# The first layer's beginning in a four-layer kernel: another load order, another engine for two norms, masks later

## The chip, the cores and the metric

The kernel runs on one core of a Trainium2 chip. The core has five engines that run side by side, each through its own instruction list in order: TensorE (PE, matrix products; its weight loads are listed as PEld), VectorE (DVE), ScalarE (ACT), GpSimd (POOL) and SyncE (SP), which here only issues DMA transfers. The metric is the device time of one execution in microseconds (us), the median of three runs.

## What is computed

A sequence of 2048 tokens with 576 features passes four layers, attention (A) and MLP (B) in turn, twice, with the same weights each time. Each layer adds its result to x.

```python
def _A_ref(x, wqkv, wo):            # linear attention, 32 heads of 18
    qkv = (x @ wqkv) -> q, k, v per head
    phi = lambda t: jnp.where(t > 0, t + 1, jnp.exp(t)) + 1e-6
    pq, pk = phi(q), phi(k)
    kv = jnp.einsum("bhsd,bhse->bhde", pk, v)
    z = jnp.einsum("bhsd->bhd", pk)
    num = jnp.einsum("bhqd,bhde->bhqe", pq, kv)
    den = jnp.einsum("bhqd,bhd->bhq", pq, z)[..., None] + 1e-6
    return (num / den) @ wo

def _B_ref(x, w1, b1, w2, b2):      # MLP, 576 -> 4608 -> 576
    h = _gelu(_layernorm(x) @ w1 + b1)
    return h @ w2 + b2

x = x + _A_ref(_layernorm(x), A_wqkv, A_wo)
x = x + _B_ref(_layernorm(x), B_w1, B_b1, B_w2, B_b2)
x = x + _A_ref(_layernorm(x), A_wqkv, A_wo)
x = x + _B_ref(_layernorm(x), B_w1, B_b1, B_w2, B_b2)
```

The layer norm subtracts the mean of a row and divides by the root of its variance plus 1e-5. Inputs, weights and the output are bfloat16.

## The kernel before

The 2048 tokens are 16 tiles of 128 rows. Weights stay in on-chip memory for the whole run. Between layers x lies in a scratch tensor x_d in HBM.

**The norm pipeline.** `LNPipe` takes a tile through numbered stages, one stage for each call of `tick`: statistics on DVE (L229, L230: half a row each; L232 joins them to mean and variance, ln_mv; L235 adds eps, ln_u), the power -0.5 on POOL (L242, ln_rstd), the product -mean * rstd on DVE (L246, ln_nmr), the normalised tile (L254 on ACT, or L258 on DVE or POOL) into one of four buffers `y_ring`, with a copy of its last 64 columns into the 64 pad columns on POOL (L260), and five transposes on PE (L267) whose result ACT (L269) or DVE (L271) copies to yT.

The features are 4.5 blocks of 128. The last block of yT has 64 true rows and 64 that come from the pad columns; in attention the weights' rows against the pad are zero (L158), in the MLP the pad is a second copy of the last 64 features.

**First half of an attention layer.** For each tile t, `kv_proj` computes the key products (L336, two halves into k_ps), phi of them (ACT reads k_ps twice, L289 and L291; DVE ends it, L292 and L294), and the value products (L344, L347 into v_ps, of which there is one buffer). ACT (L349) and DVE (L351) copy v_ps to `v_ring`, which frees it for the next tile. `kv_acc` adds tile t-1 to kvacc (L360). From t = 4 on, one query product (L366) is done for each tile. In the first layer `pre_a1_layer0` runs ahead of each tile: it loads and feeds tile t + LEAD, ticks the pipeline, and issues one piece of the later weights (`late_pieces`: wo, b1, nine of w1, six of w2).

**Second half.** Denominators, the product with wo (L450), and for each tile the residual sum on DVE (L316), its store to x_d, and a prefetch of the next x tile (L301: xbf, from the input in the first layer; L304: xo, from x_d, in the others). One group in five has its scaling on POOL (L442). Tiles of the next layer enter the norm pipeline here; those after the first four are read back from x_d (L224).

**Masks.** `build_masks` fills six constant tiles on POOL by memsets and affine selects. It is called once, by `late_pads`, at t = 2 of the first layer; the masks are first read after the last key and value product.

**What sets the order.** A scheduler places each engine's instructions by data dependence and priority; the order in the program is a wish. `chained` makes the DMAs that pass through it keep their order on SP. Each DMA also takes one of eight completion semaphores in turn, and waits until the DMA eight places earlier has landed. From the ninth tile of the first layer on, `pe` keeps PE in program order.

At the start PE runs 14 products of zeros (L157) on `ident`, which POOL has built, so that its clock is up when the first tile comes.

Of the kernel before, what the change touches and what calls it, by code (L numbers as in the profile page):

```python
# [15 lines left out]
P = 128  # L16
# [16 lines left out]
NWARM = 14  # L33


def build(tc, A_x, A_wqkv, A_wo, B_w1, B_b1, B_w2, B_b2, out, dbg=None, n_layers=4):
    nc = tc.nc
    dbg = dbg or {}
    with ExitStack() as ctx:
# [26 lines left out]
        act_dummy = const.tile([P, 1], F32, name="act_dummy")  # L66

        def build_masks():
            sel = nc.gpsimd.affine_select
            nc.gpsimd.memset(maskz[:], 1.0)  # L70
# [6 lines left out]
            nc.gpsimd.memset(z_row[:], 0.0)  # L77
            nc.gpsimd.memset(eps_row[:], 1e-6)
            nc.gpsimd.memset(one_row[:], 1.0)
            nc.gpsimd.memset(act_dummy[:], 0.0)  # L80
            sel(out=z_row[:], in_=z_row[:], compare_op=ALU.not_equal, fill=1.0,
                base=-126, pattern=[[0, 1]], channel_multiplier=1)
            nc.gpsimd.memset(head_sel[:], 1.0)
# [4 lines left out]
            nc.gpsimd.memset(quad_mask[:], 1.0)  # L88
# [4 lines left out]
            nc.gpsimd.memset(head_bc[:], 0.0)  # L93
# [64 lines left out]
        nc.gpsimd.memset(wqkv_sb[64:P, 4, :], 0.0)  # L158
# [5 lines left out]
        def late_setup():  # L164
            build_masks()
# [26 lines left out]
        def piece_b2_dma():  # L192
            nc.sync.dma_start(out=b2_bc[:], in_=B_b2.partition_broadcast(P))
# [8 lines left out]
        state = dict(ycnt=0, vcnt=0)  # L202

        class LNPipe:
# [3 lines left out]
            def feed(self, xt, t, kind, norm_eng, evac_eng="dve", load_from=None):  # L208
                self.items.append(dict(stage=(0 if load_from is None else -1), xt=xt, t=t, kind=kind,
                                       norm=norm_eng, evac=evac_eng, load=load_from))  # L210
# [4 lines left out]
            def tick(self, transposes=1):  # L215
                for it in list(self.items):
# [9 lines left out]
                    elif st == 0:  # L226
                        xt = it["xt"]
                        stt = work.tile([P, 2, 6], F32, name="ln_st", bufs=4)
                        nc.vector.bn_stats(out=stt[:, 0, :], in_=xt[:, 0:HALF])  # L229
                        nc.vector.bn_stats(out=stt[:, 1, :], in_=xt[:, HALF:D])  # L230
# [13 lines left out]
                    elif st == 2:  # L244
# [4 lines left out]
                    elif st == 3:  # L249
                        y = y_ring[state["ycnt"] % NY]  # L250
                        state["ycnt"] += 1
                        xt = it["xt"]
                        if it["norm"] == "act":
                            nc.scalar.activation(out=y[:, 0:D], in_=xt[:, 0:D], func=ACT.Identity,  # L254
                                                 scale=it["rstd"][:, 0:1], bias=it["nmr"][:, 0:1])
                        else:
                            eng = nc.vector if it["norm"] == "dve" else nc.gpsimd
                            eng.tensor_scalar(out=y[:, 0:D], in0=xt[:, 0:D], scalar1=it["rstd"][:, 0:1],  # L258
                                              scalar2=it["nmr"][:, 0:1], op0=ALU.mult, op1=ALU.add)
                        nc.gpsimd.tensor_copy(out=y[:, D:DPAD], in_=y[:, 4 * P:D])  # L260
                        it["y"] = y
                    elif st == 4:
                        y = it["y"]
                        t = it["t"]
                        tp = ps_tp.tile([P, KD, P], BF16, name="tp", tag="tp")
                        for k in range(KD):
                            pe(nc.tensor.transpose(out=tp[:, k, :], in_=y[:, k * P:(k + 1) * P], identity=ident[:]))  # L267
# [355 lines left out]
        def pre_a1_layer0(t):  # L623
# [85 lines left out]
```

## Time and profile before

| | |
|---|---|
| median of 3 runs | 812.3 us (812.2 to 812.8) |
| the profiled execution | 816.66 us, of which 814.7 us are the span of the trace |
| PE busy | 785.2 us (96%) |
| ACT, DVE, POOL busy | 352.2, 259.2, 120.6 us |
| first key product (L336) starts | 15.01 us |
| first value product (L344) starts | 17.95 us |
| query products end, second half begins | about 84 us |
| first MLP product (L549) starts | 128.98 us |

The span runs from the first to the last recorded instruction of the profiled execution. "Busy" is the time in which an engine executes an instruction; an idle time before an instruction is put down to whatever released it, and is named behind it in brackets. Times in the trace are us from the span's start.

### The profile page before, as it was taken

To read this page: it belongs to the slowest core of one execution; us is meant where nothing else is said; L and a number is where in the kernel's file an instruction comes from. 1 tells how busy PE (TensorE), PEld (TensorE's weight loads), DVE (VectorE), ACT (ScalarE), POOL (GpSimd) and SP (SyncE) were. 2 spreads that over 40 slices of the span, in tenths; PEclk is the share of its full clock that TensorE was granted. 3 is DMA by queue.
4 is the path that set the end of the run, shared out by engine and by line. 5 is a ranking of instruction groups with operands and counts; after the bars stand their busy time and mean duration, and the time that the engine had idled before them with its cause. 6 is when DMAs were issued, how large, how long until landed. Compare 5 with 4: busy or idle time off the path is not lost.

```text
span 814.7 us, 16146 instructions
## 1 busy us (share of the span) xinstructions
PE 785.2 (96%) x6806; PEld 510.1 (63%) x6812; DVE 259.2 (32%) x764; ACT 352.2 (43%) x765; POOL 120.6 (15%) x218
## 2 busy tenths in 40 slices
PE   5999979999999999999999998799999999999998
PEld 3777554477458647845877765446854774585476
DVE  4675873024303502310345468621400310010000
ACT  4788844610640371066037787274046107403610
POOL 8440131012201201210100002220210110011000
PEclk8999999999999999999999999999999999999999
DMA  9990274002101201100110006820310110011000
GB/s 218 253 327 4 80 230 151 1 31 73 45 25 65 89 1 31 59 31 1 59 60 1 1 1 202 270 83 16 89 43 2 51 57 11 2 44 44 2 23 23
DMA packets 42898, 56.92 MB, mean 70 GB/s; under 512 B 10251, under 2 KB 26891, under 8 KB 42827
## 3 DMA queue, kind: packets, MB, share of 16 engines
q1 hardware_dynamic: 42826, 55.91, 22.6%
q8 instruction: 53, 0.87, 0.4%
q14 instruction: 19, 0.15, 0.1%
HBM read 39.38 MB, written 16.52 MB: 69 GB/s over the span
## 4 chain that ended last, share of the span: by engine, by line
PE 88%; DVE 3%; ACT 3%; DMA 2%; POOL 1%; issue 1%; SPq 0%; DVEq 0%; ACTq 0%
PE m_ps L596 35%; PE h_ps L549 19%; PE hp_ps L549 15%; PE q_ps L366 5%; PE k_ps L336 4%; PE v_ps L347 2%; PE wo_ps L450 2%; PE v_ps L344 2%; PE tp L267 2%; DMA xl<-x_d 1%; PE kvacc L360 1%; DVE xn L316 1%; ACT rden_bc L440 1%; DMA xbf<-in_A_x_dram 1%; POOL ln_rstd L242 1%
## 5 line engine op out<-in xcount | busy, mean ns | idle before, releaser
L596 PE MATMUL m_ps<-w_sb,hT 128*128 128x288 bf16 x2304 | 289.8, 286 | 0.0
L596 PEld LDWEIGHTS <-hT 128*128 128x128 bf16 x2304 | 223.2, 98 | 57.9 <-issue 3.4
L549 PEld LDWEIGHTS <-w_sb 64*128 64x128 bf16 x2304 | 124.4, 94 | 136.5 <-issue 1.7
L549 PE MATMUL hp_ps<-yT,w_sb 64*128 64x512 bf16 x1152 | 178.0, 376 | 0.0
L554 ACT COPY relay_sb<-relay_sb 128x1 f32<-128x1 f32 x144 | 28.5, 198 | 282.4 <-PE h_ps L549 239.4
L549 PE MATMUL h_ps<-yT,w_sb 64*128 64x512 bf16 x1152 | 147.9, 376 | 0.0
L545 ACT ACTIVATE hT<-h_ps,b1T 128x512 bf16<-128x512 f32 x144 | 91.0, 683 | 43.9 <-PE h_ps L549 43.9
L271 DVE COPY yT<-tp 128x640 bf16<-128x640 bf16 x40 | 19.6, 490 | 272.2 <-PE tp L267 272.2
L545 ACT ACTIVATE hT<-hp_ps,b1T 128x512 bf16<-128x512 f32 x144 | 91.1, 692 | 0.0
L242 POOL TENSOR_TENSOR ln_rstd<-ln_u,neg_half 128x1 f32<-128x1 f32 x64 | 35.2, 551 | 339.6 <-DVE ln_u L235 185.6
L306 POOL TENSOR_TENSOR xo<-xo,b_bc 128x576 f32<-128x576 f32 x32 | 40.8, 1275 | 154.1 <-DMA xo<-x_d 152.9
L450 PE MATMUL wo_ps<-kvwo,pq 126*128 126x288 bf16 (+1 forms) x320 | 49.3, 301 | 13.5 <-POOL pq L442 9.4
L549 PE MATMUL h_ps<-yT,w_tail 64*128 64x512 bf16 x144 | 54.1, 376 | 0.0
L549 PE MATMUL hp_ps<-yT,w_tail 64*128 64x512 bf16 x144 | 54.1, 376 | 0.0
L366 PE MATMUL q_ps<-yT,wqkv_sb 128*126 128x512 bf16 (+1 forms) x200 | 50.0, 382 | 0.5 <-ACT phi_a L291 0.5
L450 PEld LDWEIGHTS <-pq 126*128 126x128 bf16 (+1 forms) x320 | 31.7, 102 | 28.5 <-POOL pq L442 10.8
L316 DVE TENSOR_TENSOR xbf<-m_ps,xo 128x576 bf16<-128x576 f32 x16 | 12.1, 757 | 106.9 <-PE m_ps L596 106.9
L336 PE MATMUL k_ps<-wqkv_sb,yT 128*128 128x288 bf16 x320 | 45.9, 291 | 0.0
L289 ACT ACTIVATE phi_e<-k_ps 128x288 bf16<-128x288 f32 x64 | 27.3, 427 | 36.5 <-PE k_ps L336 36.5
L260 POOL COPY y_ring<-y_ring 128x64 bf16<-128x64 bf16 x64 | 15.8, 248 | 158.1 <-DVE y_ring L258 146.2
L292 DVE TENSOR_SCALAR phi_e<-phi_e 128x288 bf16<-128x288 bf16 (+2 forms) x104 | 28.7, 276 | 29.1 <-ACT phi_e L289 28.8
L549 PEld LDWEIGHTS <-w_tail 64*128 64x128 bf16 x288 | 27.1, 94 | 17.1
(94 smaller groups left out, 670.1 us busy)
## 6 DMA issues: line engine op xcount, KB each, us to landing
x_d<-xn SPq DMA_DIRECT2D x48, 288.0 KB, 2.2
xo<-x_d SPq DMA_DIRECT2D x48, 288.0 KB, 3.0
xl<-x_d SPq DMA_DIRECT2D x24, 288.0 KB, 2.9
w_sb<-in_B_w_dram SPq DMA_DIRECT2D x6, 864.0 KB, 9.1
w_sb<-in_B_w_dram SPq DMA_DIRECT2D x9, 512.0 KB, 4.9
x<-in_A_x_dram SPq DMA_DIRECT2D x16, 144.0 KB, 3.8
xbf<-in_A_x_dram SPq DMA_DIRECT2D x16, 144.0 KB, 3.7
out_dram<-xbf SPq DMA_DIRECT2D x16, 144.0 KB, 1.8
```

What stands on the lines that cost most here:

```text
L242: nc.gpsimd.tensor_tensor(out=rstd[:], in0=it["u"][:], in1=neg_half[:], op=ALU.pow)
L289: act_last["exp"] = nc.scalar.activation(out=e[0:rows, 0:n], in_=ps_ap, func=ACT.Exp).ins.name
L292: nc.vector.tensor_scalar(out=e[0:rows, 0:n], in0=e[0:rows, 0:n], scalar1=1.0, scalar2=1e-6, op0=ALU.min, op1=ALU.add)
L306: nc.gpsimd.tensor_tensor(out=xo[:], in0=xo[:], in1=b2_bc[:], op=ALU.add)
L316: nc.vector.tensor_tensor(out=xn[:].rearrange("p (h n) -> p h n", h=2), in0=halves, in1=xo[:].rearrange("p (h n) -> p h n", h=2), op=ALU.add)
L336: pe(nc.tensor.matmul(kp[:, 0:HALF], lhsT=yT[:, k, tok], rhs=wqkv_sb[:, k, D + half * HALF: D + (half + 1) * HALF], start=(k == 0), stop=( ...
L366: pe(nc.tensor.matmul(qp[0:GR[g], :], lhsT=wqkv_sb[:, k, GO[g]:GO[g] + GR[g]], rhs=yT[:, k, c * CA:(c + 1) * CA], start=(k == 0), stop=(k ...
L450: pe(nc.tensor.matmul(wp[:, half, 0:HALF], lhsT=pq[(g, c)][0:GR[g], j * P:(j + 1) * P], rhs=kvwo[g][0:GR[g], half * HALF:(half + 1) * HALF ...
L545: act_last["gelu"] = nc.scalar.activation(out=hT[f][:, 0:CB], in_=dst[n], func=ACT.Gelu_apprx_tanh, bias=b1T[:, f:f + 1], scale=1.0).ins.name
L549: mm = pe(nc.tensor.matmul(dst[n], lhsT=wt, rhs=mv, start=(seen[n] == 0), stop=(seen[n] == 8)))
L554: relay = nc.scalar.copy(out=relay_sb[:, 1:2], in_=relay_sb[:, 0:1])
L596: pe(nc.tensor.matmul(acc[:, half, 0:HALF], lhsT=hT[f][:, j * P:(j + 1) * P], rhs=w2_sb[:, f, half * HALF:(half + 1) * HALF], start=(f == ...
```

## The change

- Loads on SP: x0 and x1, the key weights, x2 and x3, the value weights, x4, and, after the first four tiles are fed, the query weights. Before, five x tiles came first, then key and value weights in one transfer, then the query weights. LEAD is 4 instead of 6. `pre_a1_layer0` still calls `load_x0` for tile t + LEAD without looking whether it is there.
- Late pieces (wo, b1, w1, w2) start at t = 2 instead of 0. The loads of b2 and of the first layer's residual tiles (L193, L301) join the chain of loads.
- Tiles 0 and 1 are normalised on DVE, the other 14 on POOL (before: four on ACT, twelve on POOL). The statistics of tiles 2 and 3 are tied to come after a DVE norm.
- Norms on DVE and POOL compute (x - mean) * rstd directly; the product -mean * rstd remains only for norms on ACT. A tile so normalised needs one stage less.
- The pad copy is done in the MLP only. The four y buffers are zeroed at the start on DVE, and so are the pad rows of the weights, formerly on POOL.
- `build_masks` is called at t = 6 and its fills are tied behind the latest norm on POOL.
- 10 products of zeros on a zeroed y buffer instead of 14 on `ident`; one activation at the start loads ACT's table.

```diff
-NWARM = 14
+NWARM = 10
...
-        def build_masks():
+        def build_masks(after):
             sel = nc.gpsimd.affine_select
-            nc.gpsimd.memset(maskz[:], 1.0)
+
+            def fill(tile_, value):
+                tc.add_manual_dep(nc.gpsimd.memset(tile_[:], value).ins, after, NOSYNC, reason="masks are not urgent")
+
+            fill(maskz, 1.0)
...
-        for t in range(5):
-            load_x0(t)
-        chained(nc.sync.dma_start(out=wqkv_sb[:, 0:4, D:3 * D],
-                                  in_=A_wqkv[0:4 * P, D:3 * D].rearrange("(k p) n -> p k n", p=P)))
-        chained(nc.sync.dma_start(out=wqkv_sb[0:64, 4, D:3 * D], in_=A_wqkv[4 * P:D, D:3 * D]))
-        chained(nc.sync.dma_start(out=wqkv_sb[:, 0:4, 0:D],
-                                  in_=A_wqkv[0:4 * P, 0:D].rearrange("(k p) n -> p k n", p=P)))
-        chained(nc.sync.dma_start(out=wqkv_sb[0:64, 4, 0:D], in_=A_wqkv[4 * P:D, 0:D]))
-        nc.vector.memset(y_ring[NY - 1][:], 0.0)
+        def load_wqkv(part):
+            cols = slice(part * D, (part + 1) * D)
+            chained(nc.sync.dma_start(out=wqkv_sb[:, 0:4, cols],
+                                      in_=A_wqkv[0:4 * P, cols].rearrange("(k p) n -> p k n", p=P)))
+            chained(nc.sync.dma_start(out=wqkv_sb[0:64, 4, cols], in_=A_wqkv[4 * P:D, cols]))
+
+        load_x0(0)
+        load_x0(1)
+        load_wqkv(1)
+        load_x0(2)
+        load_x0(3)
+        load_wqkv(2)
+        load_x0(4)
+        for i in (NY - 1, 0, 1, 2):
+            nc.vector.memset(y_ring[i][:], 0.0)
         warm_ps = ps_h.tile([P, 512], F32, name="warm_ps", tag="h")
         for i in range(NWARM):
-            nc.tensor.matmul(warm_ps[:], lhsT=ident[:], rhs=y_ring[NY - 1][:, 0:512], start=True, stop=True)
-        nc.gpsimd.memset(wqkv_sb[64:P, 4, :], 0.0)
+            nc.tensor.matmul(warm_ps[:], lhsT=y_ring[NY - 1][:, 0:P], rhs=y_ring[NY - 1][:, 0:512], start=True, stop=True)
+        act_dummy = const.tile([P, 1], F32, name="act_dummy")
+        nc.scalar.activation(out=act_dummy[:, 0:1], in_=neg_half[:, 0:1], func=ACT.Exp)
+        nc.vector.memset(wqkv_sb[64:P, 4, :], 0.0)
...
         def late_setup():
-            build_masks()
+            build_masks(pool_last["norm"])
...
-            nc.sync.dma_start(out=b2_bc[:], in_=B_b2.partition_broadcast(P))
+            chained(nc.sync.dma_start(out=b2_bc[:], in_=B_b2.partition_broadcast(P)))
...
-                        nc.vector.bn_stats(out=stt[:, 0, :], in_=xt[:, 0:HALF])
-                        nc.vector.bn_stats(out=stt[:, 1, :], in_=xt[:, HALF:D])
+                        first = nc.vector.bn_stats(out=stt[:, 0, :], in_=xt[:, 0:HALF])
+                        second = nc.vector.bn_stats(out=stt[:, 1, :], in_=xt[:, HALF:D])
+                        if it["after"] is not None:
+                            for stats in (first, second):
+                                tc.add_manual_dep(stats.ins, dve_last["norm"], NOSYNC, reason="first tiles go first")
...
-                    elif st == 2:
+                    elif st == 2 and it["norm"] == "act":
...
-                    elif st == 3:
+                    elif st in (2, 3):
...
-                            eng.tensor_scalar(out=y[:, 0:D], in0=xt[:, 0:D], scalar1=it["rstd"][:, 0:1],
-                                              scalar2=it["nmr"][:, 0:1], op0=ALU.mult, op1=ALU.add)
-                        nc.gpsimd.tensor_copy(out=y[:, D:DPAD], in_=y[:, 4 * P:D])
+                            norm = eng.tensor_scalar(out=y[:, 0:D], in0=xt[:, 0:D], scalar1=it["mv"][:, 0:1],
+                                                     scalar2=it["rstd"][:, 0:1], op0=ALU.subtract, op1=ALU.mult)
+                            (pool_last if it["norm"] == "pool" else dve_last)["norm"] = norm.ins.name
+                        if it["kind"] == "B":
+                            nc.gpsimd.tensor_copy(out=y[:, D:DPAD], in_=y[:, 4 * P:D])
                         it["y"] = y
+                        it["stage"] = 4
+                        continue
...
-                nc.sync.dma_start(out=xo[:], in_=x_in[t * P:(t + 1) * P, :])
+                chained(nc.sync.dma_start(out=xo[:], in_=x_in[t * P:(t + 1) * P, :]))
...
-            return "act" if t < 4 else "pool"
-
-        LEAD = 6
-        nfed = 0
+            return "dve" if t < 2 else "pool"
+
+        LEAD = 4
         for t in range(LEAD):
             if t not in x0_tiles:
                 load_x0(t)
-            lnp.feed(x0_tiles.pop(t), t, "A", l0_norm_eng(t), "act")
-            nfed += 1
+            lnp.feed(x0_tiles.pop(t), t, "A", l0_norm_eng(t), "act", after=(t - 2 if t >= 2 else None))
             lnp.tick()
+        load_wqkv(0)
...
-            if late_pieces:
+            if t >= 2 and late_pieces:
                 late_pieces.pop(0)()
-            if t >= 2 and late_pads:
+            if t >= 6 and late_pads:
                 late_pads.pop(0)()
```

More of the change, by code (lines that the diff above doesn't have):

```diff
@@ L65, in build @@
         one_row = const.tile([1, P], BF16, name="one_row")
-        act_dummy = const.tile([P, 1], F32, name="act_dummy")
-        def build_masks():
+        def build_masks(after):
             sel = nc.gpsimd.affine_select
-            nc.gpsimd.memset(maskz[:], 1.0)
+            def fill(tile_, value):
+                tc.add_manual_dep(nc.gpsimd.memset(tile_[:], value).ins, after, NOSYNC, reason="masks are not urgent")
+            fill(maskz, 1.0)
             sel(out=maskz[:], in_=maskz[:], compare_op=ALU.is_ge, fill=0.0,
@@ L76, in build_masks @@
                 base=-126, pattern=[[0, 7], [0, DH]], channel_multiplier=1)
[L77 to L80, printed above, removed]
+            fill(z_row, 0.0)
+            fill(eps_row, 1e-6)
+            fill(one_row, 1.0)
             sel(out=z_row[:], in_=z_row[:], compare_op=ALU.not_equal, fill=1.0,
                 base=-126, pattern=[[0, 1]], channel_multiplier=1)
-            nc.gpsimd.memset(head_sel[:], 1.0)
+            fill(head_sel, 1.0)
             sel(out=head_sel[:], in_=head_sel[:], compare_op=ALU.is_ge, fill=0.0,
@@ L87, in build_masks @@
                 base=DH - 1, pattern=[[-126, G], [DH, H]], channel_multiplier=-1)
-            nc.gpsimd.memset(quad_mask[:], 1.0)
+            fill(quad_mask, 1.0)
             sel(out=quad_mask[:], in_=quad_mask[:], compare_op=ALU.is_ge, fill=0.0,
@@ L92, in build_masks @@
                 base=31, pattern=[[32, 4], [0, P]], channel_multiplier=-1)
-            nc.gpsimd.memset(head_bc[:], 0.0)
+            fill(head_bc, 0.0)
             hb = head_bc[:, :, 0:126].rearrange("p g (h d) -> p g h d", h=7)
@@ L202, in build @@
         state = dict(ycnt=0, vcnt=0)
+        pool_last = dict(norm=None)
+        dve_last = dict(norm=None)
         class LNPipe:
@@ L206, in __init__, with feed @@
                 self.items = []
-            def feed(self, xt, t, kind, norm_eng, evac_eng="dve", load_from=None):
+            def feed(self, xt, t, kind, norm_eng, evac_eng="dve", load_from=None, after=None):
                 self.items.append(dict(stage=(0 if load_from is None else -1), xt=xt, t=t, kind=kind,
-                                       norm=norm_eng, evac=evac_eng, load=load_from))
+                                       norm=norm_eng, evac=evac_eng, load=load_from,
+                                       after=after))
             def busy(self):
```

## The prediction

> **What bounds the kernel now.** I read the page's shares first (PE busy 785.2 of the 814.7 us span), then busy time by window, to find the 29.5 us in which PE is not busy. From 130 to 480 us PE misses only 0.22 us; the change acts on the first 60. The columns are window, its length, busy (instructions) of PE, PEld, DVE, ACT, POOL, granted clock, DMA share, GB/s:
>
> ```profile
> 10.00:15.00 5.00, 0.76 (x6) 0.60 (x7) 0.21 (x1) 1.48 (x3) 5.00 (x11) 0.62 1.06 267
> 15.00:20.00 5.00, 4.62 (x32) 3.31 (x29) 4.05 (x13) 3.37 (x7) 4.27 (x9) 0.69 1.20 165
> 20.00:25.00 5.00, 4.44 (x41) 3.54 (x42) 2.15 (x11) 3.57 (x10) 2.42 (x6) 1.00 0.71 140
> 25.00:30.00 5.00, 3.73 (x37) 3.14 (x37) 3.94 (x20) 3.38 (x9) 3.27 (x6) 1.00 0.96 278
> 30.00:35.00 5.00, 5.00 (x49) 3.90 (x47) 3.19 (x16) 3.22 (x8) 3.06 (x6) 1.00 0.95 280
> ```
>
> PE is short of work until 30 us and saturated after it: time won before 30 us shifts all that follows. The timeline (start, length, engine, line, idle before it) tells what it waits for:
>
> ```profile
> 13.18 0.23 POOL L260 COPY y_ring<-y_ring 128x64 bf16<-128x64 bf16 x1
> 13.46 0.29 PE L267 MATMUL tp<-ident,y_ring 128*128 128x128 bf16 x1 [4.50 <-POOL y_ring L260]
> 15.01 1.65 PE L336 MATMUL k_ps<-wqkv_sb,yT 128*128 128x288 bf16 x6
> 17.95 0.77 PE L344 MATMUL v_ps<-wqkv_sb,yT 128*128 128x252 bf16 x5
> 24.52 0.18 DVE L196 CAST b1T<-b_raw 128x36 f32<-128x36 bf16 x1 [2.07 <-DMA b_raw<-in_B_b_dram]
> 26.27 0.70 PE L344 MATMUL v_ps<-wqkv_sb,yT 128*128 128x252 bf16 x5 [1.74 <-DVE v_ring L351]
> 29.25 0.70 PE L344 MATMUL v_ps<-wqkv_sb,yT 128*128 128x252 bf16 x5
> ```
>
> Two stalls: a 64-column pad copy queued on POOL behind the masks (4.50 us), and the copy that frees v_ps, on DVE behind a cast that waits for b1 (1.74 us). Then tiles without a query product follow at 29.25 - 26.27 = 2.98 us. Last, DMA issues in narrow windows (KB, us from issue to landing), issued at 0.79, 3.11, 4.18, 5.76 and 15.70:
>
> ```profile
> x<-in_A_x_dram SPq DMA_DIRECT2D x1, 144.0 KB, 2.2
> wqkv_sb<-in_A_wqkv_dram SPq DMA_DIRECT2D x1, 1152.0 KB, 8.2
> wqkv_sb<-in_A_wqkv_dram SPq DMA_DIRECT2D x1, 576.0 KB, 10.0
> x<-in_A_x_dram SPq DMA_DIRECT2D x1, 144.0 KB, 9.4
> b_raw<-in_B_b_dram SPq DMA_DIRECT2D x1, 9.0 KB, 8.8
> ```
>
> Landing times follow the queue: 1872 KB by 11.3 us (five x tiles and the 1152 KB), 2808 KB by 15.2 us (tile 5), so 240 KB a us.
>
> **The change, part by part.** *Queue.* The new order of issue on SP, with KB summed: x0, x1 288; key weights 936; x2, x3 1224; value weights 1872; x4 2016; query weights 2664; x4 again 2808 (the loop loads tile t+4 unasked, and only this second copy is read); x5 2952; x6 3096; wo 3744; x7 3888; b1; x8 4041. On the old line this gives key weights 7.4, x2 8.0, x3 8.6, value weights 11.3, second x4 15.2 us. The old 1296 KB had 2304-byte rows, the new pieces 1152-byte ones: 6 to 11 us, mostly long rows, moved 333 GB/s, 12 to 18 us, short ones, 234. The 1.33 MB cost 4.0 us at the one and 5.7 at the other, so 0 to 1.7 us more. I take 0.6, nearer the low end, because the short-row query weights kept the 240 line: value weights 11.9, x4 15.8 us. SP's new waits (the query tail for the key weights, wo for the value weights) stand while some 600 KB, 2.5 us, are still queued, so DMA shouldn't run dry. b2 and three xbf loads (576 KB) leave the front, so w1 and w2 follow x sooner; b2 (first read by POOL at 99 us) and xbf (by DVE at 93) come around w2, whose last issue ended at 54 us: hidden, and 4 us each (the page's median landing) if they were late.
>
> *First tiles.* DVE: memsets 0.92 + 4 x 0.33 + 0.89 (L154's 0.33 us scaled to 864 columns; POOL's row for the same fill, 1.53, is the upper end) = 3.1 us; statistics of x0 and x1 to 4.9; the power on POOL 0.56; the norm 0.3 (L292's rows: 0.23 us at 288, 0.28 at 512 columns; above it L258's 0.58 on float32): y0 at 5.8. The table load (1.28 us) comes earlier than before and lies, as it did, under the wait for x0 and its statistics. The 10 warm matmuls end at 1.3 + 10 x 0.39 = 5.2, so the transposes follow warm. But DVE's program has the statistics of x2 ahead of y1: y1 waits for x2 (8.0 to 8.6) and comes at 9.5. PE's program has tile 1's transposes before the first key product, which so starts near 10, not 15.01; v0 near 12 to 13.
>
> *The next thing late.* On DVE the statistics of x4 stand ahead of tile 0's phi and of its v_ring copy, which v1 needs: 15.8 + 0.73 (L229, L230) + 1.5 (two L292, two L294, L232, L235, L351 at the pitch of the old rows) = 18.0. From there 2.98 us a tile: v2 at 21.0 instead of 26.27: **5.2 us won**, 3.6 (x4 at 17.4 by the slow rate) to 5.8 (x4 at 15.2). Later x tiles are ahead: x8 at 15.8 + 1233/240 + 3.2 for b1 (b1 landed 3.2 us after x7) = 24.1, needed near 25.6.
>
> *Removed work.* 56 of 64 nmr (0.21 us), 32 of 64 pad copies (0.25), four ACT norms (0.85): off PE's path after 30 us, hidden by matmuls; without cover 0.2 to 0.5 us a tile. Norms one tick earlier move transposes 24 matmuls, 3.2 us, forward in the MLP; y lies ready 7 us or more ahead (the norm at 249.29 is transposed at 260.16). Nothing.
>
> *Masks.* 8.95 us of POOL work (first read at 84 us, by the masked copy of kvacc) leaves 7.9 to 19 us and now stands behind tile 8's norm, some 28 to 37 us, ahead of tile 9's power and norm (2.0). y9 comes at 39 to 42 (24 instructions, stretched like L258's 0.82 to 1.09), due at 42. What DVE pays is shown by
>
> ```profile
> 18.00 0.97 POOL L96 TENSOR_SCALAR_AFFINE_SELECT head_bc<-head_bc 128x630 bf16<-128x630 bf16 x1
> 18.20 0.86 DVE L292 TENSOR_SCALAR phi_e<-phi_e 128x288 bf16<-128x288 bf16 x1
> 19.86 0.26 DVE L292 TENSOR_SCALAR phi_e<-phi_e 128x288 bf16<-128x288 bf16 x1
> ```
>
> 0.6 us more beside a mask. Some 15 such operations in the stretch at 0.35 are 5 us against DVE's own 1.1 us idle a tile (3.1) and 1.6 us of slack on the v copy: 0.4 us lost, bounds 0 and 3. [...]
>
> *Clock.* PE may idle 1.5 to 3 us before v1.
>
> ```profile
> 11.00:12.00 1.00, 0.00 (x0) 0.00 (x0) 0.00 (x0) 0.00 (x0) 1.00 (x3) 0.62 1.08 259
> 17.00:18.00 1.00, 1.00 (x7) 0.65 (x6) 0.44 (x3) 0.86 (x2) 1.00 (x3) 0.50 1.09 224
> 18.00:19.00 1.00, 1.00 (x10) 0.82 (x9) 0.93 (x2) 0.71 (x2) 1.00 (x3) 0.97 1.41 119
> ```
>
> Idle from 8.96, PE lost its clock 2.4 us later and had it back at 18.0, 4.5 us after work began again; half speed that long costs 2.2 us. [...]
>
> *Second half of the attention layers* (98 to 130, 495 to 520 us, 7 us idle each). POOL's program now has a power ahead of the third pq product: its 0.45 us twice, against about as much from dropped nmr. Net 0, bounds -1 and +1.
>
> Sum on the profile: 814.7 - 5.2 + 0.4 = 809.9 of span; with 1.96 outside it (816.66 - 814.7) 811.9; the profiled run is 4.4 above the median 812.3, so **807.5 us**.
>
> **Rivals.** *Clock dropped before v1*: for it the 2.4 us row, against it a slow k0 that would itself fill the gap: 809.7. *b1 holds DVE again*: for it the 2.07 us row, against it 576 KB less ahead of b1: 807.5 + 1.7 = 809.2. *More won*: x4 by the old line and the second halves at -1: 805.9. *Slower, masks beside DVE*: each phi operation at 0.86 or 0.77 instead of 0.23 or 0.31 adds 3.2 us a tile, 2.2 beyond DVE's idle time; five tiles less the slack lose 9.4: 807.1 + 9.4 = 816.5. It ends slower from four tiles on; against it, 8.95 us of masks reach over three. *The move not done*: key weights early but k0 late; in the forecast already.
>
> **How the numbers follow.** Forecast 0.62, clock 0.15, b1 0.06, more won 0.10, masks 0.07. A change within 0.2% (1.6 us) can't be told from none. Faster 0.87, same 0.07 (masks over three tiles, or clock and slow rows together), slower 0.06. The range 804.9 to 810.8 takes in both ends of x4's landing, the clock, and the second halves.
>
> **What would show it.** First k_ps near 10 us, v1 near 18 behind a v_ring copy, DVE idle for x4 up to 15.8, v2 near 21, PE full after that, masks at 28 to 40 with at most 1 us of PE idle, no idle time beyond 0.3 us from 125 to 475. It is wrong if v1 starts before 16 or after 20, or if PE stalls on y9.

## The result, and the profile after

The changed kernel takes 810.21 us (median of 20 runs, 808.32 to 813.93). The kernel before, run 20 times, took 813.96 us (811.4 to 816.52). The ratio is 0.9959, with a 95% interval of 0.9946 to 0.9972: a gain clear of the noise, though under half a per cent, of 3.3 us after the ratio and 3.75 after the medians. The profiled execution took 811.06 us with a span of 809.3 us. Set beside the old span of 814.7 that is 5.4 us less, but the old profiled run (816.66) was slower than all 20 runs of that kernel, so two spans alone would overstate the gain.

What the start won and what was given back is read from TensorE's waits in the changed kernel, 0 to 62 us. The columns are: the engine, its tile and line, who released it; the sum, how often, and the longest, in us.

```profile
PE v_ps L364 <- DVE v_ring L371: 2.6, 2, 1.9
PE tp L287 <- DVE y_ring L274: 2.5, 1, 2.5
...
PE tp L287 <- POOL y_ring L274: 0.6, 1, 0.6
```

The second line lies before the first key product. Of the first line 0.7 us is the wait before tile 1's value product (v1); the other 1.9 and the 0.6 of the last line come far later, after a stretch in which PE was full. The timeline says when (start, length, engine, line, idle before it and its releaser):

```profile
9.81 2.61 PE L356 MATMUL k_ps<-wqkv_sb,yT 128*128 128x288 bf16 x10
...
13.40 2.29 POOL L274 TENSOR_SCALAR y_ring<-x,ln_mv,ln_rstd 128x576 bf16<-128x576 bf16 x1
...
14.35 0.46 DVE L242 BATCH_NORM_STATS2 ln_st<-x 128x6 f32<-128x288 bf16 x1 [3.82 <-DMA x<-in_A_x_dram]
...
15.09 0.69 DVE L312 TENSOR_SCALAR phi_e<-phi_e 128x288 bf16<-128x288 bf16 x1
...
16.38 0.22 DVE L371 CAST v_ring<-v_ps 128x72 bf16<-128x72 f32 x1
...
16.66 0.70 PE L364 MATMUL v_ps<-wqkv_sb,yT 128*128 128x252 bf16 x5 [0.71 <-DVE v_ring L371]
...
36.83 3.11 POOL L98 TENSOR_SCALAR_AFFINE_SELECT head_bc<-head_bc 128x630 bf16<-128x630 bf16 x3
36.96 0.99 DVE L312 TENSOR_SCALAR phi_e<-phi_e 128x288 bf16<-128x288 bf16 x1
38.05 0.98 DVE L314 TENSOR_TENSOR pk<-phi_a,phi_e 128x288 bf16<-128x288 bf16 x1
...
39.69 0.21 DVE L371 CAST v_ring<-v_ps 128x72 bf16<-128x72 f32 x1
39.95 0.70 PE L364 MATMUL v_ps<-wqkv_sb,yT 128*128 128x252 bf16 x5 [1.88 <-DVE v_ring L371]
40.61 2.62 POOL L274 TENSOR_SCALAR y_ring<-x,ln_mv,ln_rstd 128x576 bf16<-128x576 bf16 x1
43.28 0.45 PE L287 MATMUL tp<-ident,y_ring 128*128 128x128 bf16 x5 [0.58 <-POOL y_ring L274]
```

Three things are to be seen. The start went as forecast in kind: x4's statistics hold DVE until 14.35, phi and the copy of v_ps follow, and v1 starts when the copy ends. The value product of tile 2 (v2) starts at 19.65 instead of 26.27: 6.6 us won. Second, the masks run from 30.92 to 39.9 us, and beside them a phi operation of DVE takes 0.98 us or so instead of 0.23 or 0.31. DVE comes late with a copy of v_ps, and behind the masks tile 9's norm comes late too: PE loses 1.88 + 0.58 = 2.46 us. Third, the norm on GpSimd takes 2.29 to 2.62 us, where the old L258 took 0.82 to 1.23. Busy time by window (us of PE, PEld, DVE, ACT, POOL; clock, DMA share, GB/s) shows how full GpSimd is:

```profile
30.00:35.00 5.00, 5.00 (x44) 3.87 (x43) 4.32 (x12) 4.27 (x12) 5.00 (x15) 1.00 1.02 293
35.00:40.00 5.00, 3.12 (x28) 2.23 (x26) 4.79 (x9) 3.67 (x9) 4.86 (x7) 1.00 0.91 272
40.00:45.00 5.00, 4.42 (x37) 3.21 (x37) 4.37 (x16) 3.17 (x7) 4.79 (x4) 1.00 0.91 275
```

Marks along the run (us; "last key product" is the last group of k_ps in the first layer):

| | before | after | difference |
|---|---|---|---|
| first key product | 15.01 | 9.81 | -5.2 |
| v2 | 26.27 | 19.65 | -6.6 |
| last key product, layer 0 | 75.44 | 71.91 | -3.5 |
| first MLP product, layer 1 | 128.98 | 123.94 | -5.0 |
| first key product, layer 2 | 417.97 | 413.20 | -4.8 |
| first MLP product, layer 3 | 525.94 | 520.38 | -5.6 |

So 3.1 of the 6.6 us are gone before the first layer's last key product. The two stalls are 2.46 us of them; the rest is in no wait that the view lists. The question for the experiments was whose fault that is: the slow norm, or the masks' new place.

### The profile page after: what moved, and what is told of

It reads as the page before. It is cut to its first block, busy times and chain, and to the rows that moved or that the text cites. A ratio compares the mean times of both kernels' runs of the same rounds, so it can differ in the third digit from the quotient of the medians.

```text
span 809.3 us, 16072 instructions
## 1 busy us (share of the span) xinstructions
PE 783.0 (97%) x6802; PEld 509.1 (63%) x6808; DVE 256.4 (32%) x714; ACT 348.8 (43%) x762; POOL 133.8 (17%) x186
## 4 chain that ended last, share of the span: by engine, by line
PE 87%; POOL 4%; ACT 3%; DVE 2%; DMA 2%; issue 2%; SPq 0%; POOLq 0%; ACTq 0%; DVEq 0%
PE m_ps L616 35%; PE h_ps L569 19%; PE hp_ps L569 15%; PE q_ps L386 4%; PE k_ps L356 4%; PE wo_ps L470 3%; PE v_ps L367 2%; PE tp L287 2%; PE v_ps L364 2%; POOL y_ring L274 2%; ACT rden_bc L460 1%; PE kvacc L380 1%; POOL ln_rstd L258 1%; DMA wqkv_sb<-in_A_wqkv_dram 1%; DVE xn L336 1%
## 5 line engine op out<-in xcount | busy, mean ns | idle before, releaser
L258 POOL TENSOR_TENSOR ln_rstd<-ln_u,neg_half 128x1 f32<-128x1 f32 x64 | 35.5, 554 | 326.4 <-DVE ln_u L251 180.0
L312 DVE TENSOR_SCALAR phi_e<-phi_e 128x288 bf16<-128x288 bf16 (+2 forms) x104 | 30.8, 297 | 31.1 <-ACT phi_e L309 30.9
L356 PEld LDWEIGHTS <-yT 128*128 128x128 bf16 x320 | 31.0, 99 | 9.3
```

Source lines behind the costliest of these rows:

```text
L258: nc.gpsimd.tensor_tensor(out=rstd[:], in0=it["u"][:], in1=neg_half[:], op=ALU.pow)
L312: nc.vector.tensor_scalar(out=e[0:rows, 0:n], in0=e[0:rows, 0:n], scalar1=1.0, scalar2=1e-6, op0=ALU.min, op1=ALU.add)
L356: pe(nc.tensor.matmul(kp[:, 0:HALF], lhsT=yT[:, k, tok], rhs=wqkv_sb[:, k, D + half * HALF: D + (half + 1) * HALF], start=(k == 0), stop=( ...
```

## The experiments

Every run below but the first (one run, for its profile only) is timed against the kernel before, on one chip within a group. Line numbers move with the edits, so the lines are read by their tiles. In the diffs, minus is the changed kernel, unless it is said that the kernel before is edited.

**1. Why the norm is slow.** Four forms by tile number, masks out of the way.

```diff
+form = it["t"] % 4 if it["norm"] == "pool" else 0
+# 0: (x - mv[:, 0:1]) * rstd     1: (x - own) * rstd, own = copy of the mean
+# 2: (x + own) * rstd, own = -mean     3: x * rstd + own, own = -mean * rstd
-            if t >= 6 and late_pads:
+            if t >= 13 and late_pads:
```

> The changed kernel with its masks moved behind the last norm on GpSimd, and the GpSimd norms of the first layer in four forms by tile number: (x - mean) * rstd with the mean read from the two-column tile ln_mv, the same with the mean in a tile of its own (ln_mean), (x + (-mean)) * rstd (ln_neg), and x * rstd + nmr (ln_nmr), so that all four run in the same surroundings. Theory (the form of the operation costs): the subtracting forms take near 2.3 us as in the changed kernel (2.29), the multiply-add form near 0.82 to 0.88 as before; the form with add first tells whether the subtraction or the order counts. Rival (VectorE beside it costs): all four take about the same, near 2.3. Rival (the two-column scalar costs): only the form that reads ln_mv takes 2.3, the other three near 0.85.

Measured, groups of instructions on GpSimd from 0 to 70 us (busy us, mean ns of one):

```profile
L290 POOL TENSOR_SCALAR y_ring<-x,ln_mean,ln_rstd 128x576 bf16<-128x576 bf16 x3 | 7.4, 2480 | 0.3
L290 POOL TENSOR_SCALAR y_ring<-x,ln_mv,ln_rstd 128x576 bf16<-128x576 bf16 x3 | 6.9, 2291 | 0.3
...
L290 POOL TENSOR_SCALAR y_ring<-x,ln_rstd,ln_nmr 128x576 bf16<-128x576 bf16 x4 | 3.8, 958 | 1.7 <-PE k_ps L372 0.8 <-issue 0.8
L290 POOL TENSOR_SCALAR y_ring<-x,ln_neg,ln_rstd 128x576 bf16<-128x576 bf16 x4 | 3.8, 958 | 0.4
```

The subtraction is what costs: both forms with it take 2.3 to 2.5 us, with or without the two-column tile; add-then-multiply costs as little as multiply-then-add. Both rivals fall. On DVE the subtracting form took 0.42 and 0.43 us in the changed kernel.

**2. The cheap norm, masks where the change has them.**

```diff
+nmr = work.tile([P, 1], F32, name="ln_nmr", bufs=4)
+nc.vector.tensor_scalar(out=nmr[:], in0=it["mv"][:, 0:1], scalar1=-1.0,
+                        scalar2=it["rstd"][:, 0:1], op0=ALU.mult, op1=ALU.mult)
-norm = eng.tensor_scalar(..., scalar1=it["mv"][:, 0:1], scalar2=it["rstd"][:, 0:1], op0=ALU.subtract, op1=ALU.mult)
+norm = eng.tensor_scalar(..., scalar1=it["rstd"][:, 0:1], scalar2=nmr[:], op0=ALU.mult, op1=ALU.add)
```

> The changed kernel with x * rstd + nmr on GpSimd again (nmr made on DVE), all else as changed, masks behind tile 8's norm. Theory (the slow norm takes the slack that the masks needed): GpSimd's norms fall from 2.29 to near 0.85 us, tile 8's norm ends some 2 us earlier or more, y9 is there before 42 us, and PE's two stalls at 39.95 and 43.28 us (1.88 and 0.58 in the changed kernel) shrink to 0.5 together: 2.0 us less than the changed kernel, ratio to the kernel before near 0.9935. Rival (the masks' place costs, whatever the form): DVE beside the selects is as late as ever, the stall of 1.9 at the v copy stays and only the 0.58 goes: ratio near 0.995.

Measured: 0.9971 (0.9955 to 0.9987). By its time that can't be told from the changed kernel's 0.9959; in the profile the last key product came later, at 74.12 instead of 71.91. The norms fell to 0.95 us and the wait on y9 went, but PE stood 3.44 us at one copy of v_ps, against 1.88. The timeline:

```profile
30.99 4.38 DVE L319 TENSOR_SCALAR phi_e<-phi_e 128x288 bf16<-128x288 bf16 x1
...
32.81 0.96 POOL L98 TENSOR_SCALAR_AFFINE_SELECT head_bc<-head_bc 128x630 bf16<-128x630 bf16 x1
...
34.32 3.04 POOL L98 TENSOR_SCALAR_AFFINE_SELECT head_bc<-head_bc 128x630 bf16<-128x630 bf16 x3
...
37.37 0.70 PE L371 MATMUL v_ps<-wqkv_sb,yT 128*128 128x252 bf16 x5 [3.44 <-DVE v_ring L378]
```

One phi operation, 0.23 us when it is alone, lasted 4.38 us. In that time GpSimd ran seven selects and fills without a gap; phi ended at 35.37, with the first of the last three head_bc selects. My theory, that the slow norm had eaten the slack, falls. The rival stands: a block of masks beside phi costs 2 to 3.4 us, whatever the norm.

**3. The same block, later.** In experiments 3 and 4 the norm is the slow one again.

```diff
-            if t >= 6 and late_pads:
+            if t >= 13 and late_pads:
```

> The changed kernel with build_masks called at t = 13 instead of 6, so that it stands behind the last norm on GpSimd (some 62 to 71 us, GpSimd idle there); the slow norm form stays. Theory (masks and slow norms together make GpSimd late): GpSimd's 2.9 us a tile alone fit the 3.0 us a tile of PE, no stall at 40 and 43, the last key product 2.4 us earlier than in the changed kernel (69.5 instead of 71.9): ratio near 0.993. Rival (the slow norms alone suffice to hold PE or DVE): a stall over 1 us remains before 60 us, ratio 0.995 or more. A cost of the new place: DVE beside the selects near 65 us may delay phi there, 0 to 0.5 us.

Measured: 0.9934 (0.9912 to 0.9957). The last key product came at 69.50, as expected, but not for the reason given. Nothing stalls at 40; the block now stands at 59.0 to 67.6 us and stalls PE there:

```profile
64.52 3.11 POOL L98 TENSOR_SCALAR_AFFINE_SELECT head_bc<-head_bc 128x630 bf16<-128x630 bf16 x3
64.64 0.99 DVE L312 TENSOR_SCALAR phi_e<-phi_e 128x288 bf16<-128x288 bf16 x1
...
66.92 0.70 PE L364 MATMUL v_ps<-wqkv_sb,yT 128*128 128x252 bf16 x5 [2.00 <-DVE v_ring L371]
```

The stall is 2.00 us instead of 2.46, although GpSimd's norms are over by then; the rest of the gain is a start that fell 1.8 us better in this execution (v2 at 17.88, x4's statistics at 13.00 instead of 14.35, with the same loads in the same order). The expectation had a cost of 0 to 0.5 us for the new place; it was 2.0.

**4. Tile 4 loaded once.**

```diff
-                load_x0(nonlocal_t)
+                if nonlocal_t not in x0_tiles:
+                    load_x0(nonlocal_t)
```

> The changed kernel without the second load of tile 4 (the first copy is used). Theory (DVE's wait for x4 sets the start of tile 1's value product): x4 lands near 12.5 instead of 14.35 us, v1 starts at 15.0 instead of 16.66, and v2 1.2 to 1.7 us earlier than 19.65; the stalls at 40 us stay or grow, as the masks stand behind an earlier norm: the last key product 0.5 to 1.5 us earlier, ratio 0.994 to 0.995. Rival (TensorE's low speed at the start sets the pace, not x4): v2 moves less than 0.4 us, ratio unchanged at 0.996.

Measured: 0.9953 (0.9935 to 0.9972). v1 started at 13.46 and v2 at 16.45, 3.2 us earlier than in the changed kernel; the last key product only 0.6 us earlier, 71.35:

```profile
38.71 2.29 POOL L274 TENSOR_SCALAR y_ring<-x,ln_mv,ln_rstd 128x576 bf16<-128x576 bf16 x1
...
41.06 0.66 PE L287 MATMUL tp<-ident,y_ring 128*128 128x128 bf16 x5 [3.60 <-POOL y_ring L274]
41.52 2.61 PE L356 MATMUL k_ps<-wqkv_sb,yT 128*128 128x288 bf16 x10
```

The norm of tile 9 ends at 41.0, set by GpSimd's queue, which runs without a listed wait from 8.66 us on: norms at 2.9 us a tile with the power, then the block. PE, earlier at the start, waits for it longer. And after this pause of 3.60 us the ten key products took 2.61 us, twice their usual 1.39; from the transposes to the second part of the value product it is 3.72 us here and 2.04 in an undisturbed tile (29.11 to 31.15), so the low rate cost 1.7 us more. Here the slow norm does count, together with the block; what the start wins is not kept.

**5. Masks in eight pieces, with the old norm and one x4.** Each piece (0.6 to 1.8 us) is tied behind the norm of one of tiles 8 to 15.

```diff
-        late_pads = [late_setup]
+        late_pads = [(lambda piece=piece: piece(pool_last["norm"])) for piece in mask_pieces()]
...
-norm = eng.tensor_scalar(..., op0=ALU.subtract, op1=ALU.mult)
+norm = eng.tensor_scalar(..., scalar1=it["rstd"][:, 0:1], scalar2=nmr[:], op0=ALU.mult, op1=ALU.add)
```

> The changed kernel with three edits: tile 4 is loaded once, GpSimd's norm is x * rstd + nmr again, and the masks are cut into eight pieces (0.6 to 1.8 us each), one behind the norm of each of tiles 8 to 15. Theory (a select holds a phi operation of DVE that falls on it, and selects back to back hold several in a row; y9 and the v copy are late because nine us of selects stand together): each piece delays one phi by up to 1 us, within DVE's idle time of a tile, so no stall over 0.3 us at 30 to 75; v2 at 16.5 as with one load of tile 4, and from there 49.6 us to the last key product as in the run with late masks less its 2.0 us stall: 66.1, 9.3 us before the kernel before, ratio near 0.989. Rival (the selects cost DVE the same wherever they stand): stalls of 2 us or more in sum remain, last key product at 68 or later, ratio 0.992 or more.

Measured: 0.9937 (0.9914 to 0.996), last key product at 71.72. The number is the rival's, but neither text had the cause. Four value products in a row, those of tiles 9 to 12 (46.06 to 60.86 us), waited 0.61 to 0.70 us each for the v copy, and a tile lasted 4.9 us instead of 4.1:

```profile
51.92 0.21 DVE L288 TENSOR_SCALAR ln_nmr<-ln_mv,ln_rstd 128x1 f32<-128x1 f32 x1 [0.67 <-POOL ln_rstd L270]
...
52.78 0.70 DVE L331 TENSOR_SCALAR phi_e<-phi_e 128x288 bf16<-128x288 bf16 x1
53.59 0.87 DVE L333 TENSOR_TENSOR pk<-phi_a,phi_e 128x288 bf16<-128x288 bf16 x1
...
55.93 0.70 PE L383 MATMUL v_ps<-wqkv_sb,yT 128*128 128x252 bf16 x5 [0.67 <-DVE v_ring L390]
```

The product nmr stands in DVE's list ahead of phi and needs GpSimd's power: DVE idles 0.67 us a tile, and then phi meets the norm and the select (0.70 and 0.87 us). That wait is what the change took away with the mean product. It also bears on experiment 2, which brought nmr back together with the cheap norm.

**6 to 8. What carried the gain at the start.** The changed kernel with the old load order (6), and the kernel before with one edit each: no pad copy in attention (7), the new load order (8).

```diff
 # 6: the changed kernel
-load_x0(0); load_x0(1); load_wqkv(1); load_x0(2); load_x0(3); load_wqkv(2); load_x0(4)
+for t in range(5): load_x0(t)
+(key and value weights in one transfer, then load_wqkv(0))
 # 7: the kernel before
-nc.gpsimd.tensor_copy(out=y[:, D:DPAD], in_=y[:, 4 * P:D])
+if it["kind"] == "B":
+    nc.gpsimd.tensor_copy(out=y[:, D:DPAD], in_=y[:, 4 * P:D])
 # 8: the kernel before, the reverse of 6
```

> The changed kernel with the load order of before (five x tiles, key and value weights in one transfer, query weights; LEAD and all else as changed). Theory of the prediction (the key weights wait behind two x tiles instead of five, and x4's second copy comes at the same place of the queue in both orders): key weights land near 11.3 instead of 7.4, the first key product starts near 11.7 instead of 9.8, but v1 still waits for x4's second copy and moves less than 1 us from 16.66: the load order alone is worth under 1 us, ratio 0.996 to 0.997. Rival (the new order is what carries the gain): v2 comes 3 us or more later than 19.65, ratio 0.999 or more.

> The kernel before with one edit: no pad copy in attention (the four y buffers zeroed on DVE instead). The 4.50 us stall of the first transposes on the pad copy goes: transposes when y0 is there (near 9 to 10 us), first key product near 11.7 instead of 15.01 when its weights land. Theory (the next thing late is another: the statistics of x5, 15.2 us, and b1's cast at 24.52, both ahead of phi and the v copy on DVE): v2 stays near 26.3, or comes at most 1.5 us earlier, ratio 0.998 to 1.000. Rival (the pad copy behind the masks carries the gain): v2 near 23 or earlier, ratio 0.996.

> The kernel before with one edit: the new load order (key weights behind x0 and x1, x2 and x3, value weights, x4, query weights). Theory (the first transposes wait for POOL's pad copy, the weights lie ready at 11.3 us in any case): the first key product stays near 15, v2 near 26.3, ratio 1.000 within 0.002. Rival (the load order carries the gain by itself): the first key product near 10, ratio 0.996.

Measured, with marks in us:

| | ratio (95%) | first key product | v2 | last key product |
|---|---|---|---|---|
| before | 1 | 15.01 | 26.27 | 75.44 |
| 6, changed, old load order | 0.9949 (0.9932 to 0.9967) | 11.34 | 20.38 | 72.59 |
| 7, before, no pad copy | 0.9984 (0.9961 to 1.0007) | 11.84 | 27.77 | 76.95 |
| 8, before, new load order | 0.9999 (0.9982 to 1.0015) | 17.95 | 26.92 | 76.09 |

The load order, first in the change's name, is worth 0.7 us at v2 against the changed kernel's profile (v2 lay between 17.88 and 19.65 in the six profiles with the new loads and two copies of x4, so 0.7 to 2.5), and nothing in the time that the runs can tell. Without it 5.9 of the 6.6 us at v2 are there. Experiment 7 shows why dropping the pad copy alone does not do it either. The first transposes came at 8.49 instead of 13.46, and then:

```profile
22.27 1.21 PE L346 MATMUL v_ps<-wqkv_sb,yT 128*128 128x252 bf16 x5 [6.00 <-DVE v_ring L353]
...
24.87 0.18 DVE L197 CAST b1T<-b_raw 128x36 f32<-128x36 bf16 x1 [1.68 <-DMA b_raw<-in_B_b_dram]
```

The 4.50 us stall that the profile before showed became one of 6.00 us: on DVE x5's statistics (15.64), two nmr that wait for powers (0.29 us, and 1.24 behind a mask), and a phi of 0.74 us beside a norm on GpSimd stand ahead of the v copy, and b1 holds DVE after that. My expectation had v2 near 26.3; it came at 27.77. In 8 the first key product came later than before, which was not expected: the first nmr stood behind the statistics of x2 and x4 on DVE, now later in the queue, and the norm of tile 0 so started at 11.47; its pad copy behind the masks came at 15.91. In the changed kernel these waits go together, and there the start is won. Which of the remaining edits (fewer tiles fed ahead, late pieces from t = 2, masks out of the first 20 us, no nmr) carries how much was not taken apart further.

**9 to 11. Pieces without the wait on the power; pieces alone; the changed kernel again.** In 9 the norm is (x + neg) * rstd, where DVE makes neg = -mean right after the mean and waits for nobody; tile 4 is loaded once. In 10 the masks are cut in pieces and nothing else is edited.

```diff
 # 9
+neg = work.tile([P, 1], F32, name="ln_neg", bufs=6)
+nc.vector.tensor_scalar(out=neg[:], in0=mv[:, 0:1], scalar1=-1.0, scalar2=None, op0=ALU.mult)
...
-norm = eng.tensor_scalar(..., scalar1=it["mv"][:, 0:1], scalar2=it["rstd"][:, 0:1], op0=ALU.subtract, op1=ALU.mult)
+norm = eng.tensor_scalar(..., scalar1=it["neg"][:], scalar2=it["rstd"][:, 0:1], op0=ALU.add, op1=ALU.mult)
 # 9 and 10
-        late_pads = [late_setup]
+        late_pads = [(lambda piece=piece: piece(pool_last["norm"])) for piece in mask_pieces()]
```

> The run with spread masks again (tile 4 loaded once, masks in eight pieces behind the norms of tiles 8 to 15), but GpSimd's norm is (x + neg) * rstd, and DVE makes neg = -mean right after the mean, so that DVE no longer waits for GpSimd's power before the product nmr. Theory (in the run before, DVE stood 0.67 us a tile waiting for the power, ahead of phi, and that is what held PE 0.6 to 0.7 us four times and stretched tiles from 4.1 to 4.9 us): GpSimd's norms 0.82 to 1.1 us, tiles at 4.1 us to the end, no stall over 0.3 us from 20 to 75 us, the last key product 49.6 us after v2, so at 66 to 69 by where x2 and x4 land; ratio 0.989 to 0.992. Rival (the selects and norms that hold phi are what costs): stalls of 0.5 us or more stay on the tiles with a head_bc select, last key product at 70 or later, ratio 0.9935 or more.

> The changed kernel with the masks spread in eight pieces behind the norms of tiles 8 to 15 and nothing else (norm by subtraction at 2.3 us, tile 4 loaded twice). Theory (the masks in one block cost 2.46 us): power 0.57, norm 2.3 and a piece of 1.1 on average are 4.0 us a tile on GpSimd against 4.1 on PE from tile 8 on: just enough, 0 to 0.7 us of stalls, last key product 69.5 to 70.2, ratio near 0.993. Rival (the slow norm and pieces together make GpSimd the bound): y late by 0.3 to 0.5 us a tile over eight tiles, 2 to 4 us of stalls on the transposes, ratio 0.996 or more.

> The changed kernel itself once more, beside the two others on the same chip, so that they can be set against it: every theory expects the ratio 0.9959 within 0.0015, and stalls near 40 and 43 us of some 2.5 us in sum. If where x2 and x4 land differs between executions, v2 moves with it, and the last key product stays near 71.9, since the block of masks takes back what comes earlier (theory: GpSimd's queue, not the start, sets y9); the rival, that an earlier start is kept, has the last key product move with v2.

| | median us | ratio (95%) | v2 | last key product | PE's waits at 20 to 75 us |
|---|---|---|---|---|---|
| 9, neg, pieces, one x4 | 806.72 | 0.9896 (0.9866 to 0.9926) | 17.78 | 67.69 | none |
| 10, pieces alone | 807.17 | 0.9901 (0.9874 to 0.9927) | 18.43 | 67.89 | none |
| 11, changed kernel | 809.79 | 0.9943 (0.9922 to 0.9963) | 19.11 | 71.37 | 1.88 and 0.59 |

Busy time of experiment 10, by window:

```profile
45.00:50.00 5.00, 5.00 (x45) 3.90 (x43) 4.17 (x13) 4.23 (x12) 4.79 (x5) 1.00 0.91 252
50.00:55.00 5.00, 5.00 (x46) 3.83 (x44) 3.90 (x15) 4.27 (x11) 4.90 (x4) 1.00 1.08 360
55.00:60.00 5.00, 5.00 (x44) 3.79 (x43) 3.21 (x13) 3.55 (x10) 4.90 (x5) 1.00 1.09 356
```

GpSimd is as full as in the changed kernel, with the same slow norms and all the masks, and PE loses nothing from 20 to 75 us. So what the change gave back was the masks' standing together; from there on the slow norm by itself costs PE nothing while GpSimd's 4.0 us a tile stay under PE's 4.1. Experiment 9 differs from 5 by neg in place of nmr alone, and the four stalls of 5 are gone, so it was the wait for the power. Experiment 10 came out better than my expectation of 0.993, which left 0 to 0.7 us of stalls and took the start from the profile with v2 at 19.65. Experiment 11 agrees with the rival in its text: v2 and the last key product moved by the same 0.5 us, so a start that falls earlier by the loads is kept there. In experiment 4, where v2 came 3.2 us earlier, it was not.

**12. Tile 1's norm ahead of x2's statistics**, on top of 9.

```diff
+            if t == 2:
+                lnp.tick()
             lnp.feed(x0_tiles.pop(t), t, "A", l0_norm_eng(t), "act", after=(t - 2 if t >= 2 else None))
```

> The run with neg and spread masks, with the norm of tile 1 placed ahead of the statistics of x2 on DVE, so that y1 does not wait for x2 to land. Theory: y1 comes near 6.7 instead of 8.6 us, and the first key product starts when its weights have landed, near 7.7 (x2, behind them in the queue, landed at 7.67 in the run before) instead of 9.23; the first value product 1.0 to 1.5 us earlier than 11.63, v2 0.5 to 1.2 us earlier than 17.78, the last key product near 66.7 instead of 67.69; ratio 0.988 to 0.990, which can't be told from the run before by its time alone. Rival (the value weights, x4 or TensorE's low speed set v1 anyway): v2 moves less than 0.4 us.

Measured: 805.23 us, 0.9882 (0.9858 to 0.9905), v2 at 16.86 (0.9 us earlier), last key product at 67.36 (0.3 earlier; a stall of 0.42 us at 23.42 on the v copy took part of it back). In place it did what was expected:

```profile
7.88 1.39 PE L376 MATMUL k_ps<-wqkv_sb,yT 128*128 128x288 bf16 x10
...
10.22 0.70 PE L384 MATMUL v_ps<-wqkv_sb,yT 128*128 128x252 bf16 x5 [0.96 <-DMA wqkv_sb<-in_A_wqkv_dram]
```

Now the weights themselves are waited for. By the first MLP product of layer 1 the lead over 9 is gone, though (119.72 against 119.59). Experiments 9, 10 and 12 can't be told from each other by time; 12 is faster than the kernel before and the changed kernel beyond the intervals.

## Why the prediction was right, and where not

**Direction and place: right.** The forecast was 807.5 us and a gain of 4.8 (5.2 won, 0.4 lost); the runs gave 810.2 and, by the medians, 3.75 (5.0 in experiment 11's group). Of the 2.7 us between the two times, 1.7 are the base: three runs had a median of 812.3, twenty have 813.96. The other 1.0 is the gain, for the most part the difference of two errors: 1.4 us more won at the start and 2.1 more lost on the masks. That these offset each other, and that the time so stayed inside the range (804.9 to 810.8), is in part luck. One of the prediction's own signs of being wrong did appear: PE stalled on y9. In its terms:

- *First tiles: right.* First key product forecast near 10, measured 9.81; y1 forecast 9.5, there at 9.24; v0 12 to 13, measured 12.21, but with key products at half rate that the text had not foreseen (2.61 us instead of 1.39). DVE did idle for x4 (3.82 us, up to 14.35) with phi queued behind it.
- *x4's landing: too late.* The forecast took 15.8 us, adding 0.6 for the short rows of the weight pieces. Its statistics began at 14.35, and at 13.0 to 14.3 in the other executions with these loads. From x2 (1080 KB by the queue, 8.09 us) to there it is 1728 KB in 6.26 us, 276 KB a us and not 240. The term for short rows has no support: with 1152-byte rows alone DMA moved 314 GB/s from 5 to 13 us, near the 333 that the text read for long rows. From x4 to v1 the forecast had 2.2 us, measured 2.31. In that stood a phi operation of 0.69 us that ended with GpSimd's slow norm (13.40 to 15.69); in experiment 10 phi took 0.22 in the same place beside a norm as long, and x4 to v1 took 1.90. What decides whether phi is held there stays open. So 6.6 us were won, above the bound of 5.8.
- *Masks: the step that failed.* The prediction put 0.4 us (0 to 3) on them, with "y9 comes at 39 to 42 (24 instructions, stretched like L258's 0.82 to 1.09), due at 42", and "at most 1 us of PE idle". The stalls were 2.46 us, inside these bounds but six times the 0.4: 1.88 at the v copy, and 0.58 on y9, which was there at 43.2 (the 0.58 goes with the cheap norm, experiment 2). The same block cost 1.84 and 0.59 in experiment 6 and 1.88 and 0.59 in 11. The mechanism was in the text (the row of 0.86 us beside a select); its size was wrong because the 15 slowed operations were set against DVE's idle time averaged over tiles. Phi operations and selects come in a row: in the changed kernel six of them in a row, 33.59 to 39.03, took 0.55 to 1.10 us each, and in experiment 2 one took 4.38. Spreading the selects (10) shows that the average would have been enough, had they been spread.
- *The new norm's price: wrong.* The text priced it by L258's row, another pair of operations. It took 2.29 us at the least. From 20 us on that cost no time by itself (10), but it took GpSimd's slack, and experiment 4 shows what that costs once PE is earlier.
- *Removed work at nothing: not quite.* For the tiles on GpSimd the mean product is a wait of DVE on GpSimd's power, 0.67 us a tile in experiment 5, hidden only while DVE has time to spare. In the later layers the first key to the last key product of layer 2 took 52.78 us in the changed kernel and the same within 0.01 in all its variants, 53.43 before and in 7 and 8; the MLP ahead of it took 289.3 instead of 289.0. That is 0.4 us won net where the forecast had none. The pad copy alone does not do it (7), nor does nmr for GpSimd's norms undo it (2 and 5); which edit does was not tested.
- *Second half of layer 0:* from the last key product to the first MLP product 53.54 us before, 52.03 after; but 51.74 in experiment 7 and 53.26 in 6. It varies by more than the difference, so nothing is read from it.
- *Clock: wrong, without a price.* The text had 10 products of zeros at 0.39 us each, the average of the old 14, end at 5.2 us and "the transposes follow warm". The views give the least, the median and the greatest time of one, in ns, before and after:

```profile
L157 PE MATMUL warm_ps<-y_ring,ident x14: 379/634/634, 3.1 to 8.2; 128*128 128x512 bf16 x14
L165 PE MATMUL warm_ps<-y_ring x10: 609/634/634, 1.3 to 5.1; 128*128 128x512 bf16 x10
```

  The fast ones of the old 14 were the last, and the ten ended before any was fast, at 5.76 us. The transposes at 6.10 and at 9.30 took 0.71 us each instead of 0.44, and the first key products ran at half rate (2.61 us instead of 1.39). The forecast's sum has no term for a drop of the clock, and the runs give no rule for one: full rate after a pause of 2.39 us in experiment 7, half after 2.48 here. It set nothing: v_ps was full at 14.45, and DVE, busy with x4 and phi, copied it at 16.38.

**The rivals.** b1 was in time (its cast did not wait). "Slower, masks beside DVE" was the right mechanism at a quarter of its price: it was worked out over five tiles, 9.4 us lost after the slack; the two stalls came to 2.46 us, for the 9 us of masks reach over no more than three tiles. "The move not done" did not come true at the first key product (9.81 us), but x4's wait behind it decided: experiment 6 lost 1.5 us at the first key product and 0.7 at v2. "More won" was right for the start (6.6 us) and not for the time, as the masks took 2.46 back. "Clock dropped before v1" had the low rate right and its price wrong: v1 waited for DVE.

## What to carry to other kernels

Work that is "not urgent" still has a price if another engine's operations last longer beside it (here phi at 0.98 us instead of 0.23): cut it into pieces and tie each to a loop turn (here 0.6 to 1.8 us a piece, tiles of 4.1 us), instead of finding one late place for the block. A stall that the profile names is the last of several: ask what stands behind it on the same engine before pricing its removal, as the pad copy's 4.50 us became 6.00 elsewhere. When an edit swaps the operations of an instruction on another engine than the one whose row you have, look for that operation's own row; where there is none, the bound is wide.

## What the runs showed of the hardware

- GpSimd, tensor-scalar on 128x576 bf16: subtract then multiply 2.29 and 2.48 us on average in experiment 1 (up to 2.62 in the changed kernel), add then multiply and multiply then add 0.96 on average (0.82 at the least). On DVE the subtracting form took 0.42 and 0.43 us.
- A DVE phi operation (128x288) took 0.23 us alone. Beside GpSimd's head_bc selects (0.97 to 1.15 us each) it took 0.99 us in the changed kernel and ended within 0.1 us of the end of one of them (35.38 to 36.37, the select to 36.29). In experiment 2 one took 4.38 us, through seven GpSimd instructions without a gap, and ended with the first of the last three selects. Whether phi ended with the next select or several later differed between executions with the same selects; what decides it stays open.
- TensorE at half rate after a short pause, but not always: the ten key products of the first tile took 2.61 us in the changed kernel and 2.56 to 2.61 in seven experiments after pauses of 2.11 (3) to 2.48 us (5), and 1.39 us after pauses of 1.33 (4) and 0.78 us (12). In experiment 7, whose fourteen products of zeros ended fast (0.38 us), the first six key products took 0.94 us, full rate, behind a pause of 2.39. Later on the rate was full after 3.44 us (2) and half after 3.60 (4). So the length of the pause alone does not decide; what does stays open.
- The granted clock can miss this: it read 1.00 in the changed kernel's window 10 to 15 us, in which products ran at half rate (2.61 us for ten); in experiment 6 it read 0.50 from 10 to 15 us, with key products as slow (2.56 us).
